# Two interleaved linear-attention and squared-ReLU layers on one core: side work of ScalarE and VectorE put elsewhere in their queues, banks and the last chunks reordered

## The chip, the cores and the metric

One Trainium2 chip; the kernel runs on one core. The time is device microseconds (us) of one execution, median of several runs; less is better. The profile shows TensorE (PE, with its weight loads as PEld), VectorE (DVE), ScalarE (ACT), GpSimd (POOL) and SyncE (SP), whose queue issues most DMAs. Each engine takes its instructions in the order of the program.

## The reference

```python
def A(x, wqkv, wo):                          # x: 1 x 2048 x 640, 32 heads of 20
    q, k, v = split_heads(x @ wqkv)
    phi = lambda t: where(t > 0, t + 1, exp(t)) + 1e-6
    pq, pk = phi(q), phi(k)
    kv = einsum("bhsd,bhse->bhde", pk, v)
    z = einsum("bhsd->bhd", pk)
    o = einsum("bhqd,bhde->bhqe", pq, kv) / (einsum("bhqd,bhd->bhq", pq, z)[..., None] + 1e-6)
    return merge_heads(o) @ wo

def B(x, w1, b1, w2, b2):                    # 640 -> 1728 -> 640
    return relu(x @ w1 + b1) ** 2 @ w2 + b2

for _ in range(2):
    x = x + A(layernorm(x), wqkv, wo)
    x = x + B(layernorm(x), w1, b1, w2, b2)
```

All is float32.

## The kernel before

A product of float32 operands is made as three (`mm3`, L319): both sides are split into a high part (ScalarE copies and rounds) and a low part (VectorE subtracts), `split`, L91 to L94. Each split is therefore one ScalarE and one VectorE instruction, and PE can start on the high part alone. Rows go in 16 tiles of 128. The order on every engine is that of the Python text (the schedule is manual); the framework adds the waits.

Stage A, per tile t (loop from L580): k product `psk` of tile t; transposed input of tile t+1 made by a 32 x 32 block transpose on VectorE (`blocks_T`, tile y, L302) and 16 block copies on ScalarE (`blocks_move`, tile z, L311, four to each of its j), then `xT_split`; Exp and Relu of the k product on ScalarE (`phi_psum`, L412, L414), their sum on VectorE (`phi_sum`); products of earlier tiles into G (`g_chunk`, with an addition on VectorE each, L444); splits of x and k; normalisation and block transpose of tile t+2; a q product, left out in tiles 6, 10, 14 (`LATE`); in layer 0 also the splits of later weights (`prep`), whose low part runs on GpSimd. PSUM pairs go round a ring of four (`ps2`).

After the loop: sum of keys, five `g_chunk`, and for the first tiles the denominator (`b_den`), division (`b_div`) and block transpose on VectorE, moves on ScalarE, and a split to `pT`. Six products `pskv` are evacuated with a mask to `kvbd` (L683), five `psM` make the block weights; four output products `pso` of group 0 follow, each with residual, statistics and normalisation (`b_x1`), then two last q products.

Stage B (loop from L1067): per group of four tiles, 14 chunks c: `fc1` into the one bank "h", `act` (Relu on ScalarE at L822, square and split on VectorE; chunk 13 also reads PSUM on VectorE, L831), and `fc2` of the chunk before. Between them stands the side work of the next group's tiles, at places "pre" (before `act`), "pe" and "post" (after `fc2`), set in `side` (L977). In group 0 of each layer, `stay` (L969) splits ten resident weight units, with raw data in four stage places. Banks: `order` (L790) gives the pairs of stage A's ring to "h", five accumulators and "po". The last chunk of the last group is `fc2_last` (L908). Other weights come through a ring of six buffers, loaded by SP in order.

Of the kernel before, what the change touches and what calls it, by code (L numbers as in the profile page):

```python
# [35 lines left out]
LATE = (6, 10, 14)  # L36
N_WARM = 23
F_BUFS = 12
# [10 lines left out]
def kernel(  # L49
# [135 lines left out]

    def split_unit(nm, c, u, raw, eng=None):

        if (nm, c) == ("w1", 13):
            raw = raw[:, : DC * FL].rearrange("p (d f) -> p d f", d=DC)
            w = u.rearrange("p (d f) -> p d f", d=DC)  # L190
            hi, lo = w[:, :, :FL], w[:, :, FL:]
        else:
            hi, lo = u[:, :D], u[:, D:]
        nc.scalar.activation(hi, raw, AF.Copy)
        (eng or nc.vector).tensor_tensor(out=lo, in0=raw, in1=hi.bitcast(F32), op=ALU.subtract)

# [3 lines left out]
    class Prep:  # L200
# [14 lines left out]
        def split(self):  # L215
            if self.raws:
                nm, c, raw = self.raws.pop(0)
                u = utile("uprep")[:, : unit_len(nm, c)]
                split_unit(nm, c, u, raw, nc.gpsimd)
                self.done.append((nm, c, u))  # L220
# [7 lines left out]
    class Units:  # L228


        def __init__(self):
            self.at = {}
            self.pairs = {}
            self.ring = [u for u in uses if u[2] not in RESIDENT]
            self.stay = [u for u in uses if u[0] == 0 and u[2] in RESIDENT]
            self.free = 0
            self.raws = []

# [25 lines left out]
        def split_stay(self):  # L264
            if self.raws:
                raw = self.raws.pop(0)
                split_unit(*self.place(), raw)

# [109 lines left out]
    for layer in range(N_LAYERS):  # L378
# [81 lines left out]
        if layer == 0:  # L460

            psw = ps2("psw")
            for _ in range(N_WARM):
                nc.tensor.transpose(psw[:, :P], ident, ident)
            a_load(0, src)
            first_loads.step(0, 5)
            a_load(1, src)
            a_stats(0)
            a_apply(0)
            first_loads.step(2, 5)  # L470
            a_trans(0, ps2("psT"))
            first_loads.step(4, 5)
            a_stats(1)
            first_loads.step(1, 5)
            a_apply(1)
            first_loads.step(3, 5)
            a_load(2, src)
        ones = ap.tile([P, P], F32, name="ones", tag="ones", bufs=1)
        nc.gpsimd.memset(ones, 1.0)
# [91 lines left out]
        for t in range(NT):  # L571
# [14 lines left out]
            if t + 1 in yza:  # L586
                blocks_move(yza[t + 1], (0, 1))
            elif t < 2 and layer == 0:
                if t == 0:
                    psq = ps2("psq")  # L590
                    proj(psq, xT[t], wk("q"), range(3))
                a_trans(t + 1, ps2("psT"))
                if t == 0:
                    proj(psq, xT[t], wk("q"), range(3, DC))
# [4 lines left out]
            if first:  # L599
                a_apply(t + 2)  # L600
            e, r = phi_psum(psk)
            if first:
# [30 lines left out]
            if layer == 0 and t >= 1:  # L633
                n = 1 + (t % 3 != 1)
                for _ in range(n):
                    prep.split()
                for _ in range(n + (t in (1, 2))):
                    prep.load()
# [16 lines left out]
        for c in range(DC):  # L655
            g_chunk(NT // 2 - 1, c)
            if c == 1:
                b_den(1)
                b_blocks(1)
        b_split(0, xtile("pT"))  # L660
        blocks_move(yzp[1], range(3))
# [10 lines left out]
        maskf = mask.rearrange("p h d -> p (h d)")  # L672
        b_den(2)
        b_blocks(2)
        for c in range(NH):
# [10 lines left out]
            if c == 0:  # L686
                blocks_move(yzp[1], (3,))
                e, rl = phi_psum(psq)
                b_load_pq(3)
            if c == 1:  # L690
                b_split(1, xtile("pT"))
            if c == NH - 1:
                phi_sum(e, rl)
                nc.sync.dma_start(pqd[NT - 3], rl)
                ring.append(q_slot)
# [9 lines left out]
        for m in range(DC):  # L705
# [15 lines left out]
            if m == 3:  # L721
                b_split(2, xtile("pT"))
            if m < 2:
                b_load_x(m)
            if m == 1:
# [11 lines left out]
        for i in range(TG):  # L737
# [9 lines left out]
            if i < 2:  # L747
                b_load_x(i + 2)
            b_x1(i, po[i])
            if i < 2:  # L750
                yzx[i] = blocks_T(xn.pop(i))
            if i == 1:
                b_split(3, xtile("pT"))
                blocks_move(yzx[0], range(4))
# [34 lines left out]
        banks = {}  # L789
        order = {slots[0]: ("h", "a0"), slots[1]: ("a1", "a2"), slots[2]: ("a3", "as"), slots[3]: ("po",)}  # L790
        for i in range(4):
# [5 lines left out]

        def fc1(g, c):
            ps = fresh("h")
            u = wu.get(g, "w1", c)  # L800
# [16 lines left out]
        def act(c, ps):  # L817

            h = bp.tile([P, 2, GT], R32, tag="h", name="h", bufs=2)
            r = bp.tile([P, GT], F32, tag="hr", name="hr", bufs=2)  # L820
# [87 lines left out]
        def fc2_last(g, h, hl):  # L908

            c = NF - 1  # L910

            def add(i):
                tile_add(g, i)
                x2_store(g, i)

            for i in (TG, 0, 1):
                fc2_tile(g, c - 1, h, i)
            fc2_tile(g, c, hl, TG)
            strip_out(g)
            fc2_tile(g, c, hl, 0)  # L920
            fc2_tile(g, c - 1, h, 2)
            strip_turn(g)
            strip_add(g)
            add(0)
            fc2_tile(g, c, hl, 1)
            add(1)
            fc2_tile(g, c, hl, 2)
            add(2)
            fc2_tile(g, c - 1, h, 3)
            fc2_tile(g, c, hl, 3)  # L930
            t = TG * g + 3
# [17 lines left out]
        def stay(c):  # L949

            nonlocal n_stage
            for _ in range(3 if c == 0 else 2 if c == 2 else 1):
                wu.split_stay()
                wu.raw_stay(stage[:, n_stage % TG])
                n_stage += 1

        def side(g):
# [4 lines left out]
            def tile_(g, i, b, d, at):  # L962
# [4 lines left out]
                at(d, "post", lambda: b_blocks(t))  # L967
                at(d, "post", lambda: blocks_move(yzp[t], (0, 1)))
                at(d + 1, "post" if i == 0 else "pre", lambda: blocks_move(yzp[t], (2, 3)))  # L969
                at(d + 1, "post", lambda: b_split(t, bp.tile([P, 2, D], R32, tag="pT", name="pT", bufs=2)))  # L970
                at(b - 3, "post", lambda: b_load_x(t))

                def o():
                    po[t] = banks.pop("po") if "po" in banks else pst("pso")
                    b_out(t, po[t])
# [68 lines left out]
        for g in range(NG):  # L1044
            for c in range(NF):
# [3 lines left out]
                h = act(c, ps)  # L1049
                if last_layer and g == NG - 1 and c == NF - 1:  # L1050
                    fc2_last(g, pend[2], h)
                    break
# [4 lines left out]
                run(g, c, "pe")  # L1057
                if g == 0 and c != 1:
                    stay(c)
                run(g, c, "post")  # L1060
                if g == 0 and c < TG:
                    f_bias(c)
                if g == 0 and c == 1:
                    stay(c)
# [39 lines left out]
```

## Time and profile before

| | us |
|---|---|
| median of 3 runs | 1400.74 (1400.62 to 1400.84) |
| profiled execution | 1400.7 |
| its span, first to last instruction | 1399.0 |
| PE busy | 1368.9 |
| VectorE busy | 859.6 |
| ScalarE busy | 784.9 |

Layer 0 runs to about 700 us, layer 1 after it; in each, stage A takes some 200 us, the passage to stage B some 65, stage B some 430. The page's 40 slices show PE at nine tenths or more in all but the last, so the profile has to be read from PE's waits: who ended each, and what that engine did meanwhile. A row of the list of waits is: engine, tile and line that waited, what ended the wait, microseconds in total, times, longest.

### The profile page before, as it was taken

To read this page: it belongs to the slowest core of one execution; us is meant where nothing else is said; L and a number is where in the kernel's file an instruction comes from. 1 tells how busy PE (TensorE), PEld (TensorE's weight loads), DVE (VectorE), ACT (ScalarE), POOL (GpSimd) and SP (SyncE) were. 2 spreads that over 40 slices of the span, in tenths; PEclk is the share of its full clock that TensorE was granted. 3 is DMA by queue.
4 is the path that set the end of the run, shared out by engine and by line. 5 is a ranking of instruction groups with operands and counts; after the bars stand their busy time and mean duration, and the time that the engine had idled before them with its cause. 6 is when DMAs were issued, how large, how long until landed. Compare 5 with 4: busy or idle time off the path is not lost.

```text
span 1399.0 us, 19815 instructions
## 1 busy us (share of the span) xinstructions
PE 1368.9 (98%) x7418; PEld 1219.3 (87%) x7418; DVE 859.6 (61%) x1375; ACT 784.9 (56%) x1893; POOL 143.3 (10%) x196
## 2 busy tenths in 40 slices
PE   9999999999999999999999999999999999999998
PEld 8999998878888888888899999988888888888886
DVE  7867867676565566443476777666766554753423
ACT  5988857566545464421457877575664564463100
POOL 2444320000000000000011111100000000000000
PEclk9999999999999999999999999999999999999999
DMA  5566464362563373275521112345535525623622
GB/s 179 189 226 212 164 214 179 102 229 104 179 220 100 119 274 106 85 279 181 188 86 57 48 48 76 104 170 191 195 104 178 198 94 188 234 86 124 232 68 94
DMA packets 79434, 213.48 MB, mean 153 GB/s; under 512 B 9962, under 2 KB 21738, under 8 KB 78698
## 3 DMA queue, kind: packets, MB, share of 16 engines
q1 hardware_dynamic: 79194, 212.01, 44.1%
q8 instruction: 59, 0.97, 0.3%
q14 instruction: 37, 0.30, 0.1%
q10 hardware_dynamic: 144, 0.20, 0.0%
HBM read 162.70 MB, written 49.48 MB: 152 GB/s over the span
## 4 chain that ended last, share of the span: by engine, by line
PE 79%; ACT 10%; DVE 9%; issue 1%; DMA 0%; POOL 0%; DVEq 0%; ACTq 0%
PE psh L810 23%; PE psa L860 17%; PE psk L325 9%; PE psq L325 9%; PE pso L325 9%; ACT z L311 6%; PE psG L325 6%; PE psas L860 4%; PE psM L711 2%; DVE y L302 1%; DVE pqt L533 1%; ACT hr L822 1%; ACT e L412 1%; ACT r L414 1%; DVE xT L94 1%
## 5 line engine op out<-in xcount | busy, mean ns | idle before, releaser
L311 ACT ACTIVATE z<-y 32x160 f32<-32x160 f32 x1424 | 476.1, 334 | 167.1 <-DVE y L302 150.5
L810 PE MATMUL psh<-xTb,u 128*128 128x512 f32 x1040 | 249.7, 391 | 6.0 <-DVE hr L831 3.5
L822 ACT ACTIVATE hr<-psh,b1sb 128x512 f32<-128x512 f32 x104 | 71.7, 689 | 314.0 <-PE psh L810 313.5
L810 PEld LDWEIGHTS psh<-xTb,u 128*128 128x128 f32 x1040 | 193.6, 188 | 48.7 <-DVE hr L831 5.2
L823 DVE TENSOR_TENSOR hr<-hr 128x512 f32<-128x512 f32 x104 | 71.1, 683 | 230.9 <-ACT hr L822 230.9
L860 PE MATMUL psa<-u,h 128*128 128x512 f32 x832 | 200.7, 389 | 0.0
L860 PEld LDWEIGHTS psa<-u,h 128*128 128x128 f32 x832 | 156.1, 188 | 32.5
L325 PE MATMUL psk<-kq,xT 128*128 128x320 f32 x960 | 150.2, 312 | 5.0 <-DVE xT L94 2.9
L810 PE MATMUL psh<-xTb,uw 128*128 128x512 f32 x600 | 145.1, 394 | 6.5 <-ACT hr L822 6.5
L325 PEld LDWEIGHTS psk<-kq,xT 128*128 128x128 f32 x960 | 143.5, 189 | 8.0 <-DVE xT L94 5.4
L325 PE MATMUL psG<-kh,xh 128*128 128x320 f32 x960 | 147.5, 310 | 0.0
L325 PE MATMUL pso<-uM,pT 128*128 128x320 f32 x960 | 145.6, 309 | 1.5 <-DVE pT L94 1.5
L325 PEld LDWEIGHTS pso<-uM,pT 128*128 128x128 f32 x960 | 142.6, 188 | 4.7 <-DVE pT L94 2.0
L325 PE MATMUL psq<-kq,xT 128*128 128x320 f32 x960 | 146.5, 309 | 0.0
L325 PEld LDWEIGHTS psG<-kh,xh 128*128 128x128 f32 x960 | 142.4, 188 | 0.3
L325 PEld LDWEIGHTS psq<-kq,xT 128*128 128x128 f32 x960 | 142.0, 188 | 0.0
L810 PEld LDWEIGHTS psh<-xTb,uw 128*128 128x128 f32 x600 | 112.9, 190 | 31.6 <-ACT hr L822 8.6
L860 PE MATMUL psa<-uw,h 128*128 128x512 f32 x480 | 115.3, 389 | 0.0
L286 POOL TENSOR_SCALAR rs<-mv 128x1 f32<-128x1 f32 x64 | 15.6, 243 | 958.0 <-DVE mv L284 958.0
L860 PEld LDWEIGHTS psa<-uw,h 128*128 128x128 f32 x480 | 90.1, 188 | 18.7
L825 DVE TENSOR_TENSOR h<-hr,h 128x512 fp32r<-128x512 f32 x104 | 72.0, 693 | 3.6
L419 DVE TENSOR_SCALAR e<-e 128x640 f32<-128x640 f32 x64 | 32.9, 514 | 64.5 <-ACT e L412 63.8
(91 smaller groups left out, 1350.6 us busy)
## 6 DMA issues: line engine op xcount, KB each, us to landing
u<-kept_w SPq DMA_DIRECT2D x136, 640.0 KB, 4.4
x<-x SPq DMA_DIRECT2D x48, 320.0 KB, 5.5
kept_w<-uprep SPq DMA_DIRECT2D x17, 640.0 KB, 4.2
pqt<-pq SPq DMA_DIRECT2D x32, 320.0 KB, 6.0
x<-xr SPq DMA_DIRECT2D x32, 320.0 KB, 4.1
pq<-r SPq DMA_DIRECT2D x28, 320.0 KB, 2.3
kept_kq<-kq SPq DMA_DIRECT2D x10, 640.0 KB, 5.6
x<-in_B_w_dram SPq DMA_DIRECT2D x20, 320.0 KB, 4.6
```

Source lines behind the costliest of these rows:

```text
L94: nc.vector.tensor_tensor(out=lo, in0=src, in1=hi.bitcast(F32), op=ALU.subtract)
L286: nc.gpsimd.tensor_scalar(rs, mv[:, 1:2], LN_EPS, None, op0=ALU.add)
L302: nc.vector.transpose(out=y, in_=src)
L311: nc.scalar.activation(zv[j * B32 : (j + 1) * B32, :, i, :], yv[i * B32 : (i + 1) * B32, :, j, :], AF.Copy)
L325: nc.tensor.matmul(ps, a, b, start=first and i == 0, stop=last and i == 2)
L419: nc.vector.tensor_scalar(e, e, 1.0, PHI_EPS, op0=ALU.min, op1=ALU.add)
L711: nc.tensor.matmul(ps[:, j * 512 : j * 512 + HD], kvbd[c][:n, o : o + P], vo["o", c][:n, j * HD : (j + 1) * HD], start=c == cs[0], stop=c ...
L810: nc.tensor.matmul(ps, a[:, d, :], bb[:, d, :], start=d == 0 and i == 0, stop=d == DC - 1 and i == len(seq) - 1,)
L822: nc.scalar.activation(r, ps, AF.Relu, bias=b1sb[:, c : c + 1])
L823: nc.vector.tensor_tensor(out=r, in0=r, in1=r, op=ALU.mult)
L825: nc.vector.tensor_tensor(out=h[:, 1], in0=r, in1=h[:, 0].bitcast(F32), op=ALU.subtract)
L860: nc.tensor.matmul(ps, l, r, start=first and k == 0, stop=last and k == len(a) - 1)
```

## The change

`N_WARM` goes from 23 to 30, and 15 more warm-up transposes follow the first real ones. Splits are cut into `split_high` and `split_low`, so that resident weights' two halves stand at different places in a chunk. In LATE tiles all moves and the split of the next tile stand before Exp and Relu; preps avoid these tiles. In the passage, denominator, division and transpose of tile 2, two x loads and the split of tile 3 change places. In stage B, the banks of `order` are handed to other pairs, the second `fc1` of a layer uses the "po" pair, the first tile of a group has its moves and split one chunk later, resident weights go one per chunk, and in the last group chunk 13's `fc1` and `act` run before `fc2` of chunk 11, with the last two chunks' `fc2` tile by tile.

```diff
@@ -34,7 +34,7 @@
...
 LATE = (6, 10, 14)
-N_WARM = 23
+N_WARM, N_WARM_2 = 30, 15
 F_BUFS = 12
@@ -183,15 +183,18 @@
...
-    def split_unit(nm, c, u, raw, eng=None):
-
+    def unit_parts(nm, c, u, raw):
         if (nm, c) == ("w1", 13):
-            raw = raw[:, : DC * FL].rearrange("p (d f) -> p d f", d=DC)
             w = u.rearrange("p (d f) -> p d f", d=DC)
-            hi, lo = w[:, :, :FL], w[:, :, FL:]
-        else:
-            hi, lo = u[:, :D], u[:, D:]
+            return w[:, :, :FL], w[:, :, FL:], raw[:, : DC * FL].rearrange("p (d f) -> p d f", d=DC)
+        return u[:, :D], u[:, D:], raw
+
+    def split_high(*unit):
+        hi, lo, raw = unit_parts(*unit)
         nc.scalar.activation(hi, raw, AF.Copy)
+
+    def split_low(*unit, eng=None):
+        hi, lo, raw = unit_parts(*unit)
         (eng or nc.vector).tensor_tensor(out=lo, in0=raw, in1=hi.bitcast(F32), op=ALU.subtract)
@@ -216,7 +219,8 @@
...
                 u = utile("uprep")[:, : unit_len(nm, c)]
-                split_unit(nm, c, u, raw, nc.gpsimd)
+                split_high(nm, c, u, raw)
+                split_low(nm, c, u, raw, eng=nc.gpsimd)
                 self.done.append((nm, c, u))
@@ -234,7 +238,7 @@
...
             self.free = 0
-            self.raws = []
+            self.raws, self.halves = [], []
@@ -264,7 +268,11 @@
...
                 raw = self.raws.pop(0)
-                split_unit(*self.place(), raw)
+                self.halves.append((*self.place(), raw))
+                split_high(*self.halves[-1])
+
+        def split_low(self):
+            split_low(*self.halves.pop(0))
@@ -459,9 +467,13 @@
...
-            psw = ps2("psw")
-            for _ in range(N_WARM):
-                nc.tensor.transpose(psw[:, :P], ident, ident)
+            psw = ps2("psw", hold=True)
+
+            def warm(n):
+                for _ in range(n):
+                    nc.tensor.transpose(psw[:, :P], ident, ident)
+
+            warm(N_WARM)
             a_load(0, src)
@@ -469,12 +481,14 @@
...
             a_trans(0, ps2("psT"))
+            warm(N_WARM_2)
             first_loads.step(4, 5)
...
             a_load(2, src)
+            ring.append(0)
         ones = ap.tile([P, P], F32, name="ones", tag="ones", bufs=1)
@@ -584,7 +598,7 @@
...
             if t + 1 in yza:
-                blocks_move(yza[t + 1], (0, 1))
+                blocks_move(yza[t + 1], range(4) if t in LATE else (0, 1))
             elif t < 2 and layer == 0:
@@ -598,6 +612,8 @@
...
                 a_apply(t + 2)
+            if t in LATE:
+                xT_split(t + 1, yza.pop(t + 1)[1])
             e, r = phi_psum(psk)
@@ -631,10 +647,11 @@
...
             if layer == 0 and t >= 1:
-                n = 1 + (t % 3 != 1)
-                for _ in range(n):
+                if t > 1 and t not in LATE:
                     prep.split()
-                for _ in range(n + (t in (1, 2))):
+                    prep.split()
+                if t + 1 not in LATE:
+                    prep.load()
                     prep.load()
@@ -657,6 +674,8 @@
...
                 b_blocks(1)
+            if c == 3:
+                b_den(2)
         b_split(0, xtile("pT"))
@@ -670,8 +689,6 @@
...
         maskf = mask.rearrange("p h d -> p (h d)")
-        b_den(2)
-        b_blocks(2)
         for c in range(NH):
@@ -688,7 +705,13 @@
...
             if c == 1:
+                b_div(2)
+                b_load_x(0)
+            if c == 2:
+                yzp[2] = blocks_T(pq.pop(2))
+            if c == 3:
                 b_split(1, xtile("pT"))
+                b_load_x(1)
             if c == NH - 1:
@@ -720,8 +743,6 @@
...
                 b_split(2, xtile("pT"))
-            if m < 2:
-                b_load_x(m)
             if m == 1:
@@ -746,11 +767,12 @@
...
                 b_load_x(i + 2)
+            if i == 1:
+                b_split(3, xtile("pT"))
             b_x1(i, po[i])
...
             if i == 1:
-                b_split(3, xtile("pT"))
                 blocks_move(yzx[0], range(4))
@@ -787,7 +809,7 @@
...
         banks = {}
-        order = {slots[0]: ("h", "a0"), slots[1]: ("a1", "a2"), slots[2]: ("a3", "as"), slots[3]: ("po",)}
+        order = {slots[1]: ("h", "a0"), slots[3]: ("po",), slots[0]: ("a1", "a2"), slots[2]: ("a3", "as")}
         for i in range(4):
@@ -795,8 +817,13 @@
...
-        def fc1(g, c):
-            ps = fresh("h")
+        def fc1(g, c, spare=False):
+            if spare:
+                ps = pst("psh")[:, :512]
+            elif g == 0 and c == 1:
+                ps = banks["po"][:, :512]
+            else:
+                ps = fresh("h")
             u = wu.get(g, "w1", c)
@@ -816,7 +843,7 @@
...
-            h = bp.tile([P, 2, GT], R32, tag="h", name="h", bufs=2)
+            h = bp.tile([P, 2, GT], R32, tag="h", name="h", bufs=3)
             r = bp.tile([P, GT], F32, tag="hr", name="hr", bufs=2)
@@ -908,26 +935,19 @@
...
             c = NF - 1
-
-            def add(i):
-                tile_add(g, i)
-                x2_store(g, i)
-
-            for i in (TG, 0, 1):
+            for i in (TG, *range(TG)):
                 fc2_tile(g, c - 1, h, i)
-            fc2_tile(g, c, hl, TG)
-            strip_out(g)
-            fc2_tile(g, c, hl, 0)
-            fc2_tile(g, c - 1, h, 2)
-            strip_turn(g)
-            strip_add(g)
-            add(0)
-            fc2_tile(g, c, hl, 1)
-            add(1)
-            fc2_tile(g, c, hl, 2)
-            add(2)
-            fc2_tile(g, c - 1, h, 3)
-            fc2_tile(g, c, hl, 3)
+                fc2_tile(g, c, hl, i)
+                if i == TG:
+                    strip_out(g)
+                if i == 0:
+                    strip_turn(g)
+                if i < TG - 1:
+                    tile_add(g, i)
+                if i == 0:
+                    strip_add(g)
+                if i < TG - 1:
+                    x2_store(g, i)
             t = TG * g + 3
@@ -949,8 +969,8 @@
...
             nonlocal n_stage
-            for _ in range(3 if c == 0 else 2 if c == 2 else 1):
-                wu.split_stay()
+            for _ in range(len(wu.halves)):
+                wu.split_low()
                 wu.raw_stay(stage[:, n_stage % TG])
@@ -965,13 +985,17 @@
...
                 at(d, "post", lambda: b_blocks(t))
-                at(d, "post", lambda: blocks_move(yzp[t], (0, 1)))
-                at(d + 1, "post" if i == 0 else "pre", lambda: blocks_move(yzp[t], (2, 3)))
-                at(d + 1, "post", lambda: b_split(t, bp.tile([P, 2, D], R32, tag="pT", name="pT", bufs=2)))
+                if i > 0:
+                    at(d, "post", lambda: blocks_move(yzp[t], (0, 1)))
+                    at(d + 1, "pre", lambda: blocks_move(yzp[t], (2, 3)))
+                else:
+                    at(d + 1, "post", lambda: blocks_move(yzp[t], (0, 1)))
+                    at(d + 2, "pre" if g == 1 else "post", lambda: blocks_move(yzp[t], (2, 3)))
+                at(*((d + 2, "pre" if g == 1 else "post") if i == 0 else (d + 1, "post")), lambda: b_split(t, bp.tile([P, 2, D], R32, tag="pT", name="pT", bufs=2)))
                 at(b - 3, "post", lambda: b_load_x(t))
...
                 def o():
-                    po[t] = banks.pop("po") if "po" in banks else pst("pso")
+                    po[t] = pst("pso")
                     b_out(t, po[t])
@@ -1047,20 +1071,24 @@
...
                 h = act(c, ps)
-                if last_layer and g == NG - 1 and c == NF - 1:
-                    fc2_last(g, pend[2], h)
+                if last_layer and g == NG - 1 and c == NF - 2:
+                    hl = act(c + 1, fc1(g, c + 1, spare=True))
+                    fc2(*pend)
+                    x1_load(g)
+                    fc2_last(g, h, hl)
                     break
...
                 run(g, c, "pe")
-                if g == 0 and c != 1:
-                    stay(c)
+                if g == 0:
+                    for _ in range(3 if c == 0 else 1):
+                        wu.split_stay()
                 run(g, c, "post")
...
                     f_bias(c)
-                if g == 0 and c == 1:
+                if g == 0:
                     stay(c)
```

## Rows read from the trace of the kernel before

**Rows 1.** Page: busy us (share of the span) and instructions of PE and others.
```profile
PE 1368.9 (98%) x7418; PEld 1219.3 (87%) x7418; DVE 859.6 (61%) x1375; ACT 784.9 (56%) x1893; POOL 143.3 (10%) x196
```

**Rows 2.** Waits of PE over the whole span: total us, times, longest.
```profile
PE psh L810 <- ACT hr L822: 9.0, 9, 2.0
PE psh L810 <- DVE hr L831: 3.5, 4, 0.9
PE psk L325 <- DVE xT L94: 2.9, 7, 0.5
PE pskv L679 <- DVE kvbd L683: 2.6, 4, 1.1
PE psk L325 <- ACT xT L93: 1.9, 3, 0.8
PE pso L325 <- DVE pT L94: 1.5, 2, 0.7
...
PE psas L860 <- DVE h L836: 1.3, 1, 1.3
```

**Rows 3.** Chain of waits, whole span: start us, us, what.
```profile
9.13 5.93 PE psk L325 x29
...
29.36 4.40 PE psk L325 x30
...
345.06 3.42 PE psh L810 x15
...
383.24 3.69 PE psh L810 x15
```

**Rows 4.** Windows: stretch, us, busy by engine, PEclk (granted), DMA share, GB/s.
```profile
9.00:12.00 3.00, 2.87 (x11) 2.87 (x12) 2.97 (x5) 2.47 (x4) 0.00 (x0) 0.50 1.04 403
288.90:292.20 3.30, 3.30 (x10) 2.52 (x9) 2.13 (x3) 3.19 (x9) 0.00 (x0) 0.50 0.99 319
978.00:981.00 3.00, 3.00 (x15) 2.48 (x14) 2.07 (x3) 2.89 (x9) 0.00 (x0) 1.00 0.94 351
```

**Rows 5.** Timeline of the start: start us, us, engine, line, operation, out<-in.
```profile
15.18 2.48 DVE L94 TENSOR_TENSOR kq<-st,kq 128x640 fp32r<-128x640 f32 x3
```

**Rows 6.** Timeline, layer 1, tiles 6 and 7; brackets: idle before, releaser.
```profile
774.97 2.75 ACT L311 ACTIVATE z<-y 32x160 f32<-32x160 f32 x8
...
779.51 2.76 ACT L311 ACTIVATE z<-y 32x160 f32<-32x160 f32 x8
...
782.30 0.74 ACT L93 ACTIVATE xT<-z 128x640 fp32r<-128x640 f32 x1
...
783.94 4.53 PE L325 MATMUL psk<-kq,xT 128*128 128x320 f32 x29 [0.37 <-DVE xT L94]
...
785.92 0.84 DVE L302 STREAM_TRANSPOSE y<-xt 128x640 f32<-128x640 f32 x1
...
794.47 0.82 DVE L94 TENSOR_TENSOR xT<-z,xT 128x640 fp32r<-128x640 f32 x1 [1.25 <-ACT xT L93]
```

**Rows 7.** Timeline, layer 0, the passage at the block weights.
```profile
216.85 2.25 DVE L444 TENSOR_TENSOR G<-psG,G 128x640 f32<-128x640 f32 x3
...
220.60 0.82 DVE L524 TENSOR_REDUCE den<-pr 128x32 f32<-128x640 f32 x1
```

**Rows 8.** Timeline, layer 0, first chunks of stage B.
```profile
271.58 3.74 PE L810 MATMUL psh<-xTb,u 128*128 128x512 f32 x15 [0.84 <-ACT hr L822]
...
283.32 2.77 ACT L311 ACTIVATE z<-y 32x160 f32<-32x160 f32 x8 [7.27 <-DVE y L302]
...
287.47 5.30 PE L810 MATMUL psh<-xTb,uw 128*128 128x512 f32 x15 [1.96 <-ACT hr L822]
```

**Rows 9.** Timeline, layer 0, chunk 13 of group 0.
```profile
379.00 2.76 ACT L311 ACTIVATE z<-y 32x160 f32<-32x160 f32 x8 [4.34 <-DVE y L302]
```

**Rows 10.** Timeline of the end: the last DMA issue.
```profile
1394.93 0.37 ACTq L935 DMA_DIRECT2D out_dram<-x  x1
```

**Rows 11.** Page: DMA issues, count, KB each, median us to landing.
```profile
u<-kept_w SPq DMA_DIRECT2D x136, 640.0 KB, 4.4
```

## The prediction: each wait of TensorE followed to what ends it

> **What bounds it now.** The page first: TensorE (PE) is busy for 98% of the span [rows 1], so its matmuls are the floor, and an edit that moves other engines' work can only win back time in which PE stands still. The list of PE's waits comes next [rows 2]: 22.7 us in seven rows, none of them a DMA. All are of one kind: a short step on ScalarE (ACT) or VectorE (DVE) that PE needs stands behind longer work in that engine's queue. The chain of waits shows what a wait costs beyond its own length: 15 matmuls take 3.42 us in steady state, 3.69 after a wait [rows 3]. So each wait is charged its length plus 0.27. The windows show a further loss: the granted clock is 0.50, 1.2 instead of 2.4 GHz, at 9 to 12 us and at 288.9 to 292.2 [rows 4], each time after PE had stood still in pieces or for 1.96 us [rows 8].
>
> The profiled execution took 1400.7 us with a span of 1399.0; the median is 1400.74. I subtract from 1400.7.
>
> **(a) Start: -0.5.** Seven more warm-up transposes end about when the first real transposes are ready, and fifteen between these and the first product fill a hole. If the clock then holds, the first product's 29 matmuls need 4.25 (29/30 of the steady 4.40) instead of 5.93 [rows 3], 1.7 less. But the third q weight is split only by the first of three subtractions that run from 15.18 to 17.66 [rows 5], so PE, 1.7 early, waits for it at about 16.1 and then takes the remaining twelve matmuls and the transposes: some 0.5 is left. Bounds: 0 (clock falls later instead) and 1.7.
>
> **(b) Tiles 6, 10, 14 (LATE): -1.0.** They have no q product to cover, so PE reaches the next tile's k product before its transposed input is split. The new order puts 16 moves and the split ahead of Exp and Relu. In layer 1, tile 6: 16 moves from 774.97 take 5.5 (two rows of eight), the split 0.74, so its first half is ready at 781.2 instead of 783.0, its second at 782.0: the wait at 783.94 goes (0.37+0.27). But Exp and Relu now end 3 us later, and VectorE's queue is strict: sum, two additions into G, two split halves, normalise, transpose. y of tile 8, ready at 786.8 [rows 6], comes 1.2 later; from there 16 moves, Exp, Relu and the split run without a hole to the subtraction ending at 795.3, which becomes 796.5. PE, 0.64 early, wants it at 795.7. The wait returns one tile later, with about 0.1 on top. In layer 0 the two waits after tile 6 shrink and grow in the same manner. Only tile 14 has no tile 16 behind it: 0.7 and 0.6 are kept. Four times +0.1 and those two make -1.0. Bounds: all LATE waits vanish (the psk rows of [rows 2], 4.8 less 1.2 of the start, and eight restarts: -6), or +1. I take the low end, since the queue of [rows 6] has no slack. The preps taken out of LATE tiles don't shorten it: layer 1 has none, and its queue is the one worked out here.
> The Trainium skill (SBUF — State Buffer, section "Who interferes with whom") says of the port pair that VectorE and GpSimd share that the one that comes second blocks fully until the other ends. By that, the sum into acc, which now starts later on GpSimd, could hold a two-input subtraction for some tenths more; the sum would be 1376.6 instead of 1376.3. No row here separates it.
>
> **(c) Block weights (pskv): -2.2.** Today the denominator, division and transpose of tile 2 stand on VectorE ahead of the first evacuation: 1.13 and 0.17 of waiting per layer, 2.6 in all [rows 2]. The new places: denominator between the fourth and fifth addition into G, division after the second evacuation, transpose after the third. What is late next: the denominator (product and reduction, 0.82 each [rows 7]) now delays the fifth G addition from 219.1 to 220.7, and the first pskv needs that at about 220.4: 0.3 returns per layer. The evacuations of chunks 2 to 5 then fall before their banks or the M products need them (last at 226.6, needed at 228). 2.6 and four restarts of about 0.1, less 0.4 per layer: 2.2. Bounds 0 and 3. The two x loads, moved ahead of a store and three ring loads in SP's queue, are used 15 us later.
>
> **(d) Split of tile 3 ahead of tile 1's residual: -2.0.** ScalarE has its half ready 6 us earlier; only VectorE's order holds it. 1.5 in two waits [rows 2] and two restarts. Tile 1's transpose comes 0.8 later, but ScalarE is still moving tile 0's blocks then.
>
> **(e) Second fc1 into the spare bank: -2.2.** It waits 0.84 for ScalarE to empty the first one's bank [rows 8]; the "po" pair is read by 268.7, before PE wants it at 270.6. 2 x (0.84+0.27).
>
> **(f) Fourth fc1: -4.5, and the clock -1.6.** ScalarE stood for 7.27 us at the moves of tile 4, waiting for y at 283.3, with the Relu that empties the bank behind them; PE waited 1.96 in each layer [rows 8]. With the moves a chunk later, that Relu runs at 280.9. 2 x (1.96+0.27) = 4.5. In layer 0 the 15 matmuls after it took 5.30 at half clock [rows 8] instead of 3.7: 1.6. What is late next: the moves, the split and the next Relu now stand in one row (283.3 to 290.3), and tile 4's output product needs the split at 291.0, when it is ready at 290.6. It fits by 0.4.
>
> **(g) The other five waits on that Relu: -3.2.** 9.0 in nine, less 2 x 0.84 and 2 x 1.96, is 3.4, with five restarts 4.75. They come from y of tiles 5 and 6 being late; the resident weights' subtraction (0.8 each) now follows the division and transpose instead of leading them, and tile 4's split is off that stretch: y comes some 2 us earlier relative to PE. The last of the five in each layer stays: between two Relus ScalarE has a weight copy, 8 moves, a split, 8 moves and the Relu, 0.73+2.76+0.74+2.76+0.69 = 7.7 [rows 6], against 6.8 on PE. I leave 0.8 twice: 3.2. Bounds 0 and 4.7.
>
> **(h) Group ends: -4.6.** Eight moves of the next group's tile (2.76 [rows 9]) stood ahead of chunk 13's short activation; PE waited 0.87 four times, 3.5 in all [rows 2], and four restarts of 0.27. Moved behind it, they have 13 us until the output product. The last group boundary has no such moves and no wait.
>
> **(i) End: -2.6.** The last fc1 runs before two second-matmul chunks instead of one, so its 3.3 us of activation is covered: 1.35 and 0.27. The outputs, which now leave ScalarE's and SP's queues in one bunch ending at 1395.3 [rows 10], spread over 4 us; the last has the DMA engines nearly alone, which I price at 1.0 by the 4.1 between its issue and the end. Bounds 1.0 and 3.3.
>
> Sum: 0.5+1.0+2.2+2.0+2.2+4.5+1.6+3.2+4.6+2.6 = 24.4, so 1400.7 - 24.4 = 1376.3.
>
> **Rivals.** *The waits come back in group 0:* (f) fits by 0.4 only, and (g) builds on it; were y 1 us later than I work out, tile 4's product and the next three fc1 would each wait about 1 again in both layers: 8 to 10 lost, 1385. For it: ScalarE is filled from 283 on [rows 8]; against: no work is added to it. Chance 0.20.
> *LATE and pskv go whole:* 5 more, 1371. Against: the queue of [rows 6]. Chance 0.10.
> *The clock falls once elsewhere:* the same 1.96 wait cost a half-clock stretch in layer 0 and none in layer 1 (1.00 at 978 [rows 4]), so a remaining wait may be hit: +1.6, 1378. The Trainium skill, TensorE: Matmul & The Clock Gate, Part 1, says that the gate's window runs free of the kernel and the number of slow matmuls varies between runs; by that the times would scatter by a microsecond, and three runs within 0.22 don't show it. Chance 0.10.
> *It doesn't do what it says:* the Relus stay behind moves merely renamed, only (d), (e) and some of (i) come, and new waits eat them: 1399. Against: each wait of [rows 2] has its blocker named in the diff. Chance 0.06.
> *Slower:* SP's queue in group 0. A resident weight's raw load waits for the subtraction, now later in the chunk, and ring loads stand behind it; one lands in 4.4 us [rows 11]. At chunks 1 to 7 of two layers, 14 times, more than 24.4/14 = 1.75 us late each turns the gain into a loss; 3 us gives 1418. Against: today the same waits block SP, and [rows 2] has no DMA. Chance 0.04.
> The forecast keeps 0.50.
>
> **Range and chances.** Bounds of (a) to (i) and the rivals: 1371 to 1386 leaves out the two last rivals and edges of others, under 2 in 10. A measurement of this kernel tells about 0.2% (2.8 us) from no change. Faster: 0.50+0.20+0.10+0.10 = 0.90; same 0.06; slower 0.04.
>
> **What would show it.** Right: PE's list without "DVE hr L831", "DVE h L836" and "DVE pT"; "ACT hr" down from nine waits to about two; granted clock 1.00 from 9 us on; "xT" waits still there, moved to the k products of tiles 8 and 12; one pskv wait per layer of about 0.3, now on G. Wrong: an "ACT hr" or "pT" wait at tile 4's output product, a DMA in the list, a second clock fall.

## The result, and the profile after

The changed kernel takes **1375.59 us** (median of 4 runs, 1375.45 to 1375.73) against 1400.74: a ratio of 0.982, with a 95% interval from 0.980 to 0.984. The forecast was 1376.3. The profiled execution took 1375.58 us with a span of 1373.8, and its span is 25.2 shorter than that of before (1399.0).

The page of the changed kernel, busy time by engine; it answers to [rows 1]:

```profile
PE 1363.1 (99%) x7440; PEld 1219.6 (89%) x7440; DVE 857.5 (62%) x1375; ACT 784.9 (57%) x1893; POOL 142.8 (10%) x196
```

VectorE, ScalarE and GpSimd do the same work in the same time as before, to within 2.1 us each. TensorE's idle time, span less busy, is 10.7 now and was 30.1. PE's own busy time fell by 5.8, although it runs 22 warm-up transposes more: the two stretches at half clock are not in this trace, and the extra time of the matmuls that start again after a wait is gone with the waits.

PE's waits in the changed kernel (total us, times, longest), all rows from 0.2 us up; they answer to [rows 2]:

```profile
PE psk L333 <- DVE xT L94: 1.8, 4, 0.5
PE psw L474 <- POOL ident masks.py:199: 1.4, 1, 1.4
PE psk L333 <- ACT xT L93: 1.2, 2, 0.6
PE psq L333 <- DVE kq L94: 1.1, 1, 1.1
PE psk L333 <- ACT r L422: 0.8, 2, 0.4
PE pskv L696 <- DVE G L452: 0.4, 2, 0.2
PE psT L304 <- DVE xt L300: 0.2, 1, 0.2
```

Five rows of [rows 2] have no answer here: "ACT hr" (9.0), "DVE hr" (3.5), "DVE kvbd" (2.6), "DVE pT" (1.5) and "DVE h" (1.3). The waits for xT are still there (3.0 in six, before 4.8 in ten). Three rows are of waits that took another's place: kq and G, which the prediction has, and r, which no step foresaw.

Windows of the changed kernel (stretch, us, busy by engine, granted clock, DMA share, GB/s), the first at the start, the others at the fourth first matmul of stage B in layers 0 and 1; they answer to [rows 4]:

```profile
9.00:12.00 3.00, 2.98 (x21) 2.80 (x20) 2.63 (x5) 2.00 (x4) 0.00 (x0) 1.00 1.04 408
...
280.00:284.00 4.00, 4.00 (x19) 3.33 (x18) 3.90 (x7) 2.88 (x10) 0.00 (x0) 1.00 1.00 383
...
959.00:963.00 4.00, 4.00 (x19) 3.31 (x18) 3.90 (x7) 3.87 (x12) 0.00 (x0) 1.00 0.94 343
```

Where [rows 4] had 0.50 twice, the clock is at its full level, 2.4 GHz, and PE is busy for all but 0.02 us.

To split the 25.2 us into terms, I lined up PE's 7395 matmuls of the two traces (warm-up left out) one by one in the order of the instructions, and took the difference of their start times. It is flat over most of the span and steps where a wait went or came. A step therefore holds a wait and its restart together. Terms (c), (d), (e) and (h) rest on these steps alone; no experiment isolates them. The table gives the steps, layer 0 and layer 1, beside the terms of the prediction (minus is a gain):

| term | predicted | measured |
|---|---|---|
| (a) start | -0.5 | 0.0 (-1.35, then +1.35) |
| (b) tiles 6, 10, 14 | -1.0 | -0.19 (+0.02, -0.21) |
| (c) block weights | -2.2 | -2.35 (-1.19, -1.16) |
| (d) split of tile 3 | -2.0 | -1.98 (two of -0.99) |
| (e) second fc1 | -2.2 | -2.3 (two of -1.15) |
| (f) fourth fc1, and the clock | -6.1 | -5.75 (two of -2.25, clock -1.6, two of +0.17) |
| (g) other five waits | -3.2 | -4.89 (-1.62, -3.27) |
| (h) group ends | -4.6 | -4.68 (four of -1.17) |
| (i) end | -2.6 | -2.97 |
| small steps at the end of layer 0 | | -0.04 |
| sum | -24.4 | -25.15 |

The clock of (f) and the waits of (g) are not separate gains: what the clock took in layer 0 is what (g) is smaller by there (1.6). The last section shows why.

### The profile page after: what moved, and what is told of

It is laid out like the page before. It is cut to its first block, busy times and chain, and to the rows that moved or that the text cites. A ratio compares the mean times of both kernels' runs of the same rounds, so it can differ in the third digit from the quotient of the medians.

```text
span 1373.8 us, 19815 instructions
## 1 busy us (share of the span) xinstructions
PE 1363.1 (99%) x7440; PEld 1219.6 (89%) x7440; DVE 857.5 (62%) x1375; ACT 784.9 (57%) x1893; POOL 142.8 (10%) x196
## 5 line engine op out<-in xcount | busy, mean ns | idle before, releaser
L837 PE MATMUL psh<-xTb,u 128*128 128x512 f32 x1010 | 241.3, 390 | 0.0
L837 PEld LDWEIGHTS psh<-xTb,u 128*128 128x128 f32 x1010 | 188.4, 188 | 38.6 <-ACT hr L849 0.3
L565 DVE TENSOR_TENSOR xr<-pso,xr 128x640 f32<-128x640 f32 x32 | 26.2, 820 | 64.2 <-PE pso L333 63.9
```

The lines of the kernel that those rows point to most:

```text
L565: nc.vector.tensor_tensor(out=v, in0=halves(ps), in1=v, op=ALU.add)
L837: nc.tensor.matmul(ps, a[:, d, :], bb[:, d, :], start=d == 0 and i == 0, stop=d == DC - 1 and i == len(seq) - 1,)
```

## Experiments

Each undoes one part, does one part alone, or moves one thing more. They were timed in two later comparisons, in which the kernel before took 1400.85 and 1400.68, so a difference from the changed kernel (1375.59) is good to some tenths. Theory: the terms are waits behind longer work in an in-order queue, each worth its length and its restart, and what remains in stage A is VectorE's queue order. Rivals: the order in the LATE tiles is worth more than its steps show; the warm-up is worth its whole price; the resident subtraction's place is worth nothing.

**The LATE order undone.** The first eight moves only ahead of Exp and Relu, the split after them, as before.

```diff
-                blocks_move(yza[t + 1], range(4) if t in LATE else (0, 1))
+                blocks_move(yza[t + 1], (0, 1))
...
-            if t in LATE:
-                xT_split(t + 1, yza.pop(t + 1)[1])
             e, r = phi_psum(psk)
```

> The changed kernel (1375.6 us) with tiles 6, 10 and 14 in the old order: eight moves, Exp and Relu, eight moves, split; the new places of the preps stay. Theory (the wait is handed on to the k product of tile t+2, only tile 14 keeps it): 1375.6 to 1376.2, that is 0 to 0.6 slower, with xT waits back at the k products of tiles 7, 11 and 15. Rival (the LATE order is worth the waits that it removes): about 6 us slower, 1381.

Measured 1375.36 (1374.59 to 1376.22), ratio to the kernel before 0.982 (0.980 to 0.983): no difference from the changed kernel. In its list of PE's waits the xT rows come to 3.6 in eight, against 3.0 in six and 0.8 on r in the changed kernel; the wait on r is gone:

```profile
PE psk L333 <- DVE xT L94: 2.5, 6, 0.4
...
PE psk L333 <- ACT xT L93: 1.1, 2, 0.5
```

So the new order gave nothing by itself that these runs can tell; it moved the waits from tiles 7, 11, 15 to tiles 8 and 12. By PE's positions this run is even 0.6 shorter in these tiles, and its profile loses that much at the start, where it has a second wait for kq (0.56).

**VectorE's order mended.** If the wait came back at tile 8 because tile 8's normalisation and transpose stand behind the sums and additions of tile 6, putting them ahead must take it away.

```diff
             if t in LATE:
                 xT_split(t + 1, yza.pop(t + 1)[1])
+                if t + 2 < NT:
+                    a_apply(t + 2)
+                    yza[t + 2] = blocks_T(xt[t + 2])
...
-            if not first and not early:
+            if not first and not early and t not in LATE:
                 a_apply(t + 2)
-            if t + 2 < NT and not first and not early:
+            if t + 2 < NT and not first and not early and t not in LATE:
                 yza[t + 2] = blocks_T(xt[t + 2])
```

> The changed kernel with one more move: in tiles 6 and 10 VectorE normalises and transposes tile t+2 right after the split of tile t+1, ahead of the sum of Exp and Relu, the additions into G and the splits of x and k. Theory (the handed-on wait comes from y of tile t+2 being late on VectorE): the waits at the k products of tiles 8 and 12 go, about 1.5 each in layer 0 and 0.7 each in layer 1, so 3 to 4.5 faster, 1371.1 to 1372.6. Rival (ScalarE is full there whatever VectorE does): no change, 1375.6, or a wait at the next tile.

Measured 1370.94 (1370.75 to 1371.3), ratio 0.979 (0.977 to 0.980), 4.65 less than the changed kernel. All of its PE waits:

```profile
PE psw L474 <- POOL ident masks.py:199: 1.4, 1, 1.4
PE psk L333 <- ACT r L422: 0.8, 2, 0.4
PE psq L333 <- DVE kq L94: 0.6, 1, 0.6
PE pskv L699 <- DVE G L452: 0.4, 2, 0.2
```

The xT waits are gone altogether. The timelines of VectorE around tile 6 of layer 1, first of the changed kernel, then of this one (start us, us, engine, line, operation, out<-in), show why:

```profile
771.61 0.83 DVE L428 TENSOR_TENSOR r<-e,r 128x640 f32<-128x640 f32 x1
772.35 1.55 DVE L452 TENSOR_TENSOR G<-psG,G 128x640 f32<-128x640 f32 x2
773.82 0.96 DVE L94 TENSOR_TENSOR xh<-xt,xh 128x640 fp32r<-128x640 f32 x1
774.70 0.81 DVE L94 TENSOR_TENSOR kh<-r,kh 128x640 fp32r<-128x640 f32 x1
775.43 0.60 DVE L300 TENSOR_SCALAR xt<-xt,mv,rs 128x640 f32<-128x640 f32 x1
776.07 0.84 DVE L310 STREAM_TRANSPOSE y<-xt 128x640 f32<-128x640 f32 x1
...
784.62 0.83 DVE L94 TENSOR_TENSOR xT<-z,xT 128x640 fp32r<-128x640 f32 x1 [0.90 <-ACT xT L93]
```

```profile
767.89 0.61 DVE L300 TENSOR_SCALAR xt<-xt,mv,rs 128x640 f32<-128x640 f32 x1
768.53 0.84 DVE L310 STREAM_TRANSPOSE y<-xt 128x640 f32<-128x640 f32 x1
769.30 0.45 DVE L427 TENSOR_SCALAR e<-e 128x640 f32<-128x640 f32 x1
769.85 0.82 DVE L428 TENSOR_TENSOR r<-e,r 128x640 f32<-128x640 f32 x1
770.59 1.55 DVE L452 TENSOR_TENSOR G<-psG,G 128x640 f32<-128x640 f32 x2
...
779.02 0.83 DVE L94 TENSOR_TENSOR xT<-z,xT 128x640 fp32r<-128x640 f32 x1 [0.75 <-ACT xT L93]
```

Both are read against the k product of tile 7, which PE starts at 772.27 in the changed kernel and at 769.13 here. Tile 8's transpose starts 3.80 after it in the changed kernel and 0.60 ahead of it here; tile 8's input is ready 13.18 and 10.72 after it. PE asks for it 12.37 after it (784.64 in the changed kernel), so it waits in the one and not in the other.

**Group 0 as before.** The moves and the split of each layer's tile 4 at their old chunks, all else new.

```diff
-                if i > 0:
+                if i > 0 or g == 1:
...
-                    at(d + 1, "pre", lambda: blocks_move(yzp[t], (2, 3)))
+                    at(d + 1, "post" if i == 0 else "pre", lambda: blocks_move(yzp[t], (2, 3)))
...
-                at(*((d + 2, "pre" if g == 1 else "post") if i == 0 else (d + 1, "post")), ...
+                at(*((d + 2, "post") if i == 0 and g > 1 else (d + 1, "post")), ...
```

> The changed kernel with the moves and split of the first tile of group 1 (done in group 0 of each layer) at their old places, one chunk earlier; the group ends and the resident weights' halves stay as changed. Theory (the 1.96 wait of the fourth first-matmul chunk comes from the moves standing ahead of the Relu): +2.2 in each layer, 1380, up to 1382 if the clock falls to half once more. Rival (the order of the resident weights' halves freed it): under 1 us slower.

Measured 1384.76 (1384.39 to 1384.79), ratio 0.989 (0.987 to 0.990): 9.2 more than the changed kernel, where 4.4 to 6.4 was expected. Its PE timeline at the fourth fc1 of layers 0 and 1 (in brackets: idle before, releaser), and its windows there:

```profile
285.02 5.18 PE L837 MATMUL psh<-xTb,uw 128*128 128x512 f32 x15 [2.28 <-ACT hr L849]
...
967.30 5.29 PE L837 MATMUL psh<-xTb,uw 128*128 128x512 f32 x15 [2.31 <-ACT hr L849]
```

```profile
285.00:288.00 3.00, 2.98 (x7) 2.40 (x8) 1.81 (x3) 2.90 (x8) 0.00 (x0) 0.50 1.02 336
967.20:970.00 2.80, 2.70 (x7) 2.13 (x8) 1.81 (x3) 2.71 (x9) 0.00 (x0) 0.54 1.00 384
```

The wait is back, where it was. It is 2.3 instead of 1.96 because PE now comes there earlier, and behind it the clock falls in both layers of this trace: 15 matmuls take 5.2 and 5.3 instead of 3.4. Per layer that is 2.3 + 1.8 = 4.1; the steps in PE's positions are 4.1 and 4.2, and small ones of 0.3 at the start and 0.3 and 0.2 later make up the rest. But the second fall is not why the expectation was missed: of the four runs two show a mean granted clock of 0.998 (1384.79 and 1384.74) and two of 1.000 (1384.77 and 1384.39), so runs without a recorded fall take as long. That the old places cost 4.6 per layer and not 2.2 is shown; what PE waits for behind them when the clock stays up is in no trace, and that part of the cause stays open.

**The resident weights' order undone.** The low half's subtraction ahead of division and transpose again.

```diff
                         wu.split_stay()
+                    stay(c)
                 run(g, c, "post")
                 if g == 0 and c < TG:
                     f_bias(c)
-                if g == 0:
-                    stay(c)
```

> The changed kernel (1375.6) with one edit undone: the low half of the resident weights is subtracted on VectorE ahead of the division and transpose of the chunk again, 0.8 us in each chunk of group 0. Theory: y of tiles 5 and 6 comes 0.8 to 2 us later against TensorE, ScalarE's moves and the Relu behind them with it, and with 0.9 us of slack found at the fc1 of chunk 7 the waits on that Relu come back in part: one to two waits per layer of 0.3 to 0.8 and 0.27 each, 1 to 3 us more, 1376.6 to 1378.6. Rival: that order is worth nothing, because tile 4's split being moved already gives y the time: 1375.6, no wait on the Relu in the list.

Measured 1380.05 (1379.9 to 1380.58), ratio 0.985 (0.984 to 0.987): 4.5 more, over the range expected, and the rival that it is worth nothing falls. Its list of PE's waits has this row again:

```profile
PE psh L837 <- ACT hr L849: 3.1, 4, 1.1
```

The steps are 1.4 and 0.7 in each layer, at the fc1 of chunks 7 and 8, with 0.1 in front of them. ScalarE's timeline there, the changed kernel first, then this one:

```profile
305.54 0.69 ACT L849 ACTIVATE hr<-psh,b1sb 128x512 f32<-128x512 f32 x1
...
311.12 5.53 ACT L319 ACTIVATE z<-y 32x160 f32<-32x160 f32 x16 [3.64 <-DVE y L310]
316.68 0.69 ACT L849 ACTIVATE hr<-psh,b1sb 128x512 f32<-128x512 f32 x1
```

```profile
307.08 0.69 ACT L849 ACTIVATE hr<-psh,b1sb 128x512 f32<-128x512 f32 x1
...
313.40 5.54 ACT L319 ACTIVATE z<-y 32x160 f32<-32x160 f32 x16 [4.38 <-DVE y L310]
318.96 0.69 ACT L849 ACTIVATE hr<-psh,b1sb 128x512 f32<-128x512 f32 x1
```

The same 16 moves and the Relu behind them come 2.28 later, while PE's matmuls are at nearly the same place in both (0.17 apart) up to there. VectorE's block transposes of tiles 4, 5 and 6 start at 280.23, 291.56 and 310.25 in the changed kernel and 0.80, 1.54 and 2.27 later here: each chunk's subtraction adds its own 0.7 to 0.8, and ScalarE's row of moves carries the sum on.

**The start as before.** 23 warm-up transposes and none between.

```diff
-N_WARM, N_WARM_2 = 30, 15
+N_WARM, N_WARM_2 = 23, 0
```

> The changed kernel (1375.6) with the start as before: 23 warm-up transposes, none between the first transposes and the first product. Theory: the 1.35 us that the warm-up wins at the end of the first product is lost again 0.6 us later, where the third chunk of the q product waits 1.1 for its split weight; so no difference, 1375.3 to 1375.9, with the wait on kq shorter by about 1.1 and the granted clock low near 9 to 12 us. Rival: the warm-up is worth its full price, 1.7 more, 1377.3. A clock that falls later for want of it would show as more than that.

Measured 1375.76 (1375.49 to 1376.0), ratio 0.982 (0.981 to 0.984): no difference. In its profile the clock is low again, and the wait for kq is not in its list:

```profile
9.00:12.00 3.00, 3.00 (x13) 3.00 (x14) 2.63 (x4) 2.14 (x4) 0.00 (x0) 0.58 1.04 398
```

**The third q weight first.**

```diff
-            first_loads.step(1, 5)
+            first_loads.step(2, 5)
             a_apply(1)
-            first_loads.step(3, 5)
+            first_loads.step(2, 5)
```

> The changed kernel with the third q weight's split ahead of the normalisation of tile 1 at the start. Theory (the warm-up's gain of 1.35 is lost to the wait for that split, since VectorE stands idle for 0.78 ahead of the normalisation): 1.0 to 1.4 faster, 1374.2 to 1374.6. Rival (the start is bound by the loads, which fill the DMA engines to 15 us): no change, 1375.6.

Measured 1374.81 (1374.68 to 1375.22), ratio 0.982 (0.980 to 0.983), 0.8 less. The wait for kq is gone. The gain is less than the wait, and no larger than what runs of one kernel differ by (1.6 in the first experiment), but the four runs here lie below all four of the changed kernel. The one profile has its first real transposes at 7.67, the changed kernel's at 6.63.

**Both together.** The edits of the second and of the last experiment.

> The changed kernel with two more edits of order: in tiles 6, 10 and 14 the tile after the next is normalised and transposed right after the next one's split, ahead of the sums and additions into G (alone 1370.9), and at the start the third q weight is split ahead of the first tile's normalisation (alone 1374.8). Theory: they touch different stretches and add, 1370.9 less 0.5 to 1.3, so 1369.6 to 1370.4, and TensorE's list keeps only the small waits on r and G, about 1.2 in sum beside the first one. Rival: what is won at the start is taken back at the first k product's wait, 1370.9.

Measured **1369.88** (1369.52 to 1370.55), ratio 0.978 (0.977 to 0.980): the best of the kernels here. Of the expected 0.5 to 1.3 over the second experiment, 1.1 shows in the medians. Its profiled run has a wait for kq of 0.59, since VectorE there stood 0.82 waiting for a weight's first half; how much the start keeps is not settled by one profile.

**The end alone, on the kernel before.**

```diff
-                if last_layer and g == NG - 1 and c == NF - 1:
-                    fc2_last(g, pend[2], h)
+                if last_layer and g == NG - 1 and c == NF - 2:
+                    hl = act(c + 1, fc1(g, c + 1, spare=True))
+                    fc2(*pend)
+                    x1_load(g)
+                    fc2_last(g, h, hl)
```

(with the new `fc2_last` and a third buffer for h)

> The kernel before (1400.7) with one part of the change alone: the last fc1 ahead of the second matmul of the chunk before it, and the last two chunks tile by tile. Theory: the end is independent of all else and gives what it gave in the whole change, 3.0: 1397.8, from 1397.4 to 1398.2; the wait before the last second matmul is gone and the last output is issued some 3 us before the span ends instead of 4.1. Rival: the spread of the outputs gives nothing, and only the wait and its restart, 1.6, are won: 1399.1.

Measured 1397.35 (1397.08 to 1397.64), ratio 0.998 (0.997 to 0.999): 3.3 less than the kernel before in the same comparison (1400.68). The last output's issue, here and in the changed kernel:

```profile
1392.87 0.37 ACTq L928 DMA_DIRECT2D out_dram<-x  x1
```

```profile
1370.78 0.37 ACTq L955 DMA_DIRECT2D out_dram<-x  x1
```

The spans end at 1395.9 and 1373.8: 3.0 after the issue in both, 4.1 before [rows 10]. So spreading the outputs gave 1.1, and the rest, 2.0, is the earlier issue.

## Why the prediction was right, and where it was not

The mechanism held for the waits of stage B and the passage: each of [rows 2] went when its blocker was moved, and was worth its length and about 0.3. In stage A the waits for xT moved on, as forecast. The price of the clock did not hold (under (f)). (d), (e) and (h) came within 0.1, (c) within 0.2. The part-alone run of (i) and the undone part of (f) show that these are causes, not accompaniment. The total is 0.7 off, and that is partly luck. Five terms were off by more than a quarter microsecond, (a), (b) and (f) by 1.7 in all short of the forecast, (g) and (i) by 2.1 over it:

- **(a)** The step "some 0.5 is left" failed. The full clock brings 1.35, and PE then waits 1.07 for the third q weight and restarts. The subtraction that ends that wait starts at 15.58 where [rows 5] had 15.18, since VectorE stood 0.37 earlier for ScalarE's half of another weight. That 0.4 is nearly all of the 0.5. The run without the warm-up shows that nothing is left of it; the run with the weight first shows where it went. The end-alone run adds that the warm-up is not what decides: it has the old 23 transposes, yet in its profile the clock held (29 matmuls in 4.52), and the same wait of 1.07 took the gain.
- **(b)** The returning wait was foreseen, at the right tile and by the right queue. Its size was not: y of tile 8 starts its transpose 1.8 later against PE than in [rows 6] (776.07, and PE is 11.65 ahead), not 1.2, so each pair loses 0.21 to 0.38, not 0.1. With tile 14 keeping its 0.7 and 0.6, that is 0.8 less gain than forecast, 0.1 of it a slip in the sum (0.7 and 0.6 less four times 0.1 is 0.9). The two orders run against each other settle the cause: with the change's order undone, nothing is lost; with y first, 4.65 more is won. The prediction's bound that all LATE waits vanish was thus reachable, but by VectorE's order, which the change left alone.
- **(f)** The wait went whole, and what I called "fits by 0.4" fitted: PE's output product of tile 4 has no wait. A small one came in front of it that I had not seen, 0.17 per layer. The second chunk's h is late: its Relu ends at 272.70, but VectorE squares it only at 276.98, behind six other steps, three resident subtractions among them, and PE now comes 1.1 sooner. The 1.6 for the clock, counted as a gain of its own, is a step that failed. The slow matmuls are gone from the trace, but without the fall the kernel before stands 1.6 longer, restart included, for the next two Relus (last section), and its two runs at a mean granted clock of 1.000 took 1400.69 and 1400.86. The gain belongs to (g).
- **(g)** With the clock's 1.6 the waits themselves were worth 6.5, 3.25 in each layer, against 3.2 forecast and 4.75 as the most. The step that "the last of the five in each layer stays" failed. I set 7.7 of ScalarE's work against 6.8 of PE's and left 0.8. But the Relu of chunk 6 ends at 317.37 in the changed kernel and PE wants its bank at 318.27, 0.90 of slack that I had put at 0. The next Relu ends 7.53 later (324.90), PE comes 6.79 later (325.06), and 0.16 is left. The run with the resident order undone shows how thin it is: 2.28 of delay comes out as steps of 2.25 in each layer.
- **(i)** The outputs were taken at 1.0 and gave 1.1; the rest was taken at 1.6 and gave 1.9. The run of the end alone gave the same 3.1 in its span.

Of the rivals, the waits did not come back in group 0, but the resident run shows how near that was: 2.28 of delay cost 4.5 of the 8 to 10. A clock that falls once elsewhere shows in none of the four runs (mean granted clock 1.000 in each). No wait of PE in the list was ended by a DMA.

## What to carry to other kernels

Look for the wait's blocker in the in-order queue of the engine that releases it, and when it is moved, follow the next thing that the same queue feeds: the LATE order served tile 7 and delayed tile 8 by about the same amount, and only putting the producer of the longest chain (normalise, transpose) ahead of the sums that nobody waits for removed both waits. A gain at the start of a chain counts only as far as the next input is ready: the full clock's 1.35 was given back whole some 2 us later. The same goes for a loss: a stretch at half clock cost nothing where PE would have waited behind it anyway. Where one engine's row of work fits by tenths, undo each edit that it leans on; here a subtraction of 0.8 per chunk in the wrong place cost 4.5.

## What the runs showed of the hardware

**The clock's fall does not keep its place, and in the kernel before it costs nothing in the end.** In the profile of the kernel before, 1.96 us of standing were followed by half clock in layer 0 and by full clock in layer 1 [rows 4, 8]. The run of the end alone has the same program up to the last chunks, and in its profile it is the other way round. PE's timeline at the fourth fc1 of layers 0 and 1, and at the first product of the start, in that run:

```profile
287.72 3.69 PE L810 MATMUL psh<-xTb,uw 128*128 128x512 f32 x15 [1.96 <-ACT hr L822]
...
976.56 5.29 PE L810 MATMUL psh<-xTb,uw 128*128 128x512 f32 x15 [1.97 <-ACT hr L822]
...
9.39 4.52 PE L325 MATMUL psk<-kq,xT 128*128 128x320 f32 x29 [0.45 <-DVE xT L94]
```

PE's waits for the Relu from that fc1 to chunk 7, layer 0 (280 to 330 us) and layer 1 (970 to 1020 us), first in the kernel before, then in the run of the end alone:

```profile
PE psh L810 <- ACT hr L822: 2.6, 2, 2.0
PE psh L810 <- ACT hr L822: 3.9, 3, 2.0
```

```profile
PE psh L810 <- ACT hr L822: 3.8, 3, 2.0
PE psh L810 <- ACT hr L822: 2.5, 2, 2.0
```

Where the clock falls, 15 matmuls take 1.6 longer, and PE then waits 1.3 less, with one restart of 0.3 fewer: the two traces step 1.6 apart in each layer and are together again, to within 0.2, two waits later. The times bear it out. Of the 13 runs of the kernel before in the second comparison, seven show a mean granted clock of 0.997 (median 1400.68) and six of 0.998 to 1.000 (median 1400.66). The Trainium skill (TensorE: Matmul & The Clock Gate, Part 1) says that the number of slow matmuls varies between runs of one kernel; these traces agree, also at the start, where 29 matmuls took 5.93 [rows 3] and 4.52 behind the same 23 transposes. That the runs do not scatter by a microsecond, which the prediction took as a sign against it, comes from the waits that take up the difference.

**The start varies between executions, and little of it reaches the end.** In the profiles of five kernels whose program is the same up to there (the changed kernel and the first, second, third and fourth experiment), PE's first real transposes begin at 6.63, 6.56, 7.28, 6.58 and 7.35 us, and those of the second tile at 17.54, 18.14, 17.53, 17.82 and 17.59 in the same order: the two that began latest are not behind.
